# An attention backward pass on one core: sums of Z in halves, Z behind the transposes in two iterations, row factors later, one more transposed block moved

## The chip, the cores and the metric

The kernel runs on one core of a Trainium2 chip, in one launch. The metric is the device time of that core in microseconds. Three runs of the kernel before took 2179.84, 2180.33 and 2181.2 us; the median is 2180.33 us.

## What is computed

The kernel returns the output of one layer and the gradients of its inputs and weights. The layer is an attention (32 heads of 16 channels, 2048 positions, model width 512) gated by a small MLP:

```python
def _fwd_reference(A_x, A_wqkv, A_wo, B_x, B_w1, B_b1, B_w2, B_b2):
    x = A_x
    xn = _layernorm(x, axis=-1)
    s = _A_ref(xn, A_wqkv, A_wo)        # attention, H = 32, Dh = 16, softmax over 2048 keys
    g = _silu(_B_ref(xn, B_w1, B_b1, B_w2, B_b2))
    return x + s * g

def reference(A_x, A_wqkv, A_wo, B_w1, B_b1, B_w2, B_b2, B_x, grad_out):
    ...
    _out, _vjp = jax.vjp(_f, A_x, A_wqkv, A_wo, B_w1, B_b1, B_w2, B_b2)
    _grads = _vjp(grad_out)
    _out0 = jnp.asarray(_out)
    return (_out0, *[jnp.asarray(_g) for _g in _grads])
```

The part that the change touches is the attention core: for each head the scores, their exponentials, the attention output, and the gradients of queries, keys and values, without the 2048 x 2048 matrices ever going to memory whole.

## The kernel before, in words

Three stages follow each other: a first one (class Pre) with projections, layer norms and the MLP, the attention core (attention_core, from line 1051), and a last one (class Grads) with the weight gradients. In the trace the attention core takes from about 218 us to 1852 us.

The attention core has 64 **blocks**, one for each pair of heads (16) and chunk of 512 queries (4). A block has 16 **iterations**, one for each 128 keys. The loop at line 1364 runs over g = 16 * block + iteration; "iteration 5" below means g % 16 == 5. The order of instructions on every engine is the order in which this loop emits them; nothing reorders them. In iteration g TensorE does, in this order:

- `d` and `s` (lines 1137 and 1115): two products of 32 rows by 128 columns each, d (the gradient of the probabilities) for iteration g, s (the scores) for iteration g+1. The four start nearly together, in different row groups of the array, in the order d, s, s, d. There is one buffer for s and there are three for d.
- `Z` (line 1334, emit_z at 1387): four products of 128 rows by 32 columns. They add up the gradients of keys and values of an older block, eight iterations for one half of its keys (z_unit, line 1096). ZOFF = -20 says how far Z trails: unit g - 20. There is one buffer for Z.
- `X` (lines 1232, 1235, 1239): three groups of four products of 128 rows by 32 (17) columns, for iteration g-1. The last group ("g", line 1239) reads `gts`, which VectorE makes. In iteration 1 the "g" group is put off to iteration 2.
- `tT` (lines 1192 and 1196): transposes of 128 x 128 for iteration g-1, seven of them as a rule. `cut` (line 1176) leaves out three in steps 0 and 5 of a block, where two transposes of `xs` (line 1266) take their place in the same buffer; `OLDER` (line 1174) says in which later step each block left out is made up for, as an eighth transpose. There is one buffer for tT.

ScalarE does in each iteration the exponential of s(g+1) (line 1124) and then the copy of the transposes tT of step g-1 into `ek` (line 1208). VectorE does two products gts = d * ets (line 1155, in emit_mult, hj = 0 and hj = 1), and between them at certain iterations a copy of X (emit_xs, iteration 0) or the sum of Z into `acc` (emit_acc, lines 1346 and 1348, iterations 3 and 11 with ZOFF = -20). Ahead of the two products stand the copy of a made-up block into `ek` (emit_cO, line 1215, two iterations after its step's number in OLDER), and in iterations 2 and 7 the copy of transposed xs (line 1274) with, in iteration 2, the reciprocal of the row sums `rL` (line 1294). GpSimd copies one block of ets into gts (line 1153) and makes the row factors W1, W2 that are the weights of Z, and the block's outputs (emit_fin, lines 1295 to 1313). The sync engine's queue transposes gts into `gk` by DMA (line 1172).

After the last block the loop goes on for 20 more iterations that hold the rest of Z and a few products of the last stage (tail_mid).

Of the kernel before, what the change touches and what calls it, by code (L numbers as in the profile page):

```python
# [11 lines left out]
ALU = mybir.AluOpType  # L12
# [1038 lines left out]
def attention_core(ctx, ctx_r, tc, k, grads, Oall, dQall, dKVT_out, ident_f32, ident_bf, npairs=16, nqc=4):  # L1051
    nc = tc.nc
# [37 lines left out]
    blk = [dict(Gk={}, Ek={}) for _ in range(NB)]  # L1090
    cur = {}

    def a_unit(g):
        return (g // 16, g % 16) if 0 <= g < NSTEP else None

    def z_unit(g):
        j = g // 16
        m = g % 8
        return (j, (g % 16) // 8, m if m < 4 else 7 - m, m // 4) if 0 <= j < NB else None
# [41 lines left out]
    def emit_mult(g):  # L1141
        a = a_unit(g)
        if a is None:
            emit_xs(g - 1)
            emit_acc(g + ZOFF)
            return
        kb = a[1]
        if kb % 2 == 0:
            cur["gts"] = gtp.tile([128, 2, 9, 128], bf16, name="gts")
        gts = cur["gts"]  # L1150
        st_gt[g] = gts
        b = 7 * (1 - kb // 4 % 2)
        nc.gpsimd.tensor_copy(out=gts[:, kb % 2, 8, :], in_=st_et[g][:, b // 2, b % 2, :])  # L1153
        for hj in range(2):
            nc.vector.tensor_tensor(out=gts[:, kb % 2, 4 * hj:4 * hj + 4, :],  # L1155
                                    in0=st_d.pop((g, hj))[:].rearrange("k (b q) -> k b q", b=4),
                                    in1=st_et[g][:, :, hj, :], op=ALU.mult)
            if hj == 0:
                emit_xs(g - 1)
                emit_acc(g + ZOFF)  # L1160

    def emit_dmat(g):
        a = a_unit(g)
# [7 lines left out]
            gk = blk[j]["Gk"][kc][:, kb % 4 - 1:kb % 4 + 1]  # L1171
            nc.sync.dma_start_transpose(out=gk.rearrange("q r x k -> q (r x) k"), in_=st_gt[g][:].rearrange("k a x q -> k (a x q)"))

    OLDER = {4: (0, 0), 6: (0, 1), 7: (0, 2), 8: (5, 0), 12: (5, 1), 13: (5, 2)}

    def cut(g):
        return 3 if g >= 16 and g % 16 in (0, 5) else 0

    def older(g):
        return OLDER.get(g % 16) if 16 <= g < NSTEP else None  # L1180

# [91 lines left out]
        j, h = f  # L1273
        nc.vector.tensor_copy(out=blk[j]["xs"][:, 256 * h:256 * h + 256], in_=blk[j].pop("XT"))

    def emit_fin(g):
        f = fin_half(g)
        if f is None:
            return
        j, half = f  # L1280
        p, qc = blocks[j]
        NQq = k.op0["NATQq"]
        NQd = k.op0["NATQd"]
        xf = blk[j]["xs"][:]
        XE = xf[:, 0:256].rearrange("q (b h c) -> q b h c", b=4, h=2)
        XG = xf[:, 256:512].rearrange("q (b h c) -> q b h c", b=4, h=2)
        W1, W2 = WT[j % 2]
        st0 = qc * 4
        nqs = NQq[:, st0:st0 + 4, :, :]
        ndo = NQd[:, st0:st0 + 4, :, :]  # L1290
        bc = lambda ap: ap.to_broadcast([128, 4, 2, 16])
        if half == 1:
            rL = finp.tile([128, 4, 2, 1], f32, name="rL")
            nc.vector.reciprocal(out=rL[:], in_=XG[:, :, :, 17:18])  # L1294
            nc.gpsimd.tensor_tensor(out=W2[:, :, :, 16:32], in0=nqs, in1=bc(rL[:]), op=ALU.mult)  # L1295
            ndl = finp.tile([128, 4, 2, 1], f32, name="ndl")
            nc.gpsimd.tensor_tensor(out=ndl[:], in0=XG[:, :, :, 0:1], in1=rL[:], op=ALU.mult)
            ndr = finp.tile([128, 4, 2, 1], f32, name="ndr")
            nc.gpsimd.tensor_tensor(out=ndr[:], in0=ndl[:], in1=rL[:], op=ALU.mult)
            nc.gpsimd.tensor_tensor(out=W1[:, :, :, 0:16], in0=ndo, in1=bc(rL[:]), op=ALU.mult)  # L1300
            nc.gpsimd.tensor_tensor(out=W1[:, :, :, 16:32], in0=nqs, in1=bc(ndr[:]), op=ALU.mult)
            blk[j]["r"] = rL, ndl
            return
        rL, ndl = blk[j].pop("r")
        Ov = Oall[:, st0:st0 + 4, p * 32:(p + 1) * 32].rearrange("q b (h c) -> q b h c", h=2)
        nc.gpsimd.tensor_tensor(out=Ov, in0=XE[:, :, :, 16:32], in1=bc(rL[:]), op=ALU.mult)
        t1 = finp.tile([128, 4, 2, 16], f32, name="t1")
        nc.gpsimd.tensor_tensor(out=t1[:], in0=XE[:, :, :, 0:16], in1=bc(ndl[:]), op=ALU.mult)
        nc.gpsimd.tensor_tensor(out=t1[:], in0=XG[:, :, :, 1:17], in1=t1[:], op=ALU.add)
        rL4 = finp.tile([128, 4, 2, 1], f32, name="rL4")  # L1310
        nc.gpsimd.tensor_scalar(out=rL4[:], in0=rL[:], scalar1=0.25, scalar2=None, op0=ALU.mult)
        dQv = dQall[:, st0:st0 + 4, p * 32:(p + 1) * 32].rearrange("q b (h c) -> q b h c", h=2)
        nc.gpsimd.tensor_tensor(out=dQv, in0=t1[:], in1=bc(rL4[:]), op=ALU.mult)
        blk[j].pop("xs")

    def emit_z(g):
        u = z_unit(g)
        if u is None:
            return
        j, kp, qb, part = u  # L1320
        if part == 0 and qb == 0:
            blk[j]["Z"] = ps_z.tile([128, 512], f32, name="Z", tag="z")
        Z = blk[j]["Z"]
        for par in range(2):
            kc = 2 * kp + par
            for hj in range(2):
                r = 64 * par + 32 * hj
                if part == 0:
                    mv = blk[j]["Gk"][kc][:, :, 4 * hj + qb, :]
                elif 2 * qb + hj == 7 * (1 - par):  # L1330
                    mv = blk[j]["Gk"][kc][:, :, 8, :]
                else:
                    mv = blk[j]["Ek"][kc][:, :, 2 * qb + hj - par, :]
                nc.tensor.matmul(Z[r:r + 32, :], lhsT=WT[j % 2][1 - part][:, qb, hj, :], rhs=mv,  # L1334
                                 start=(part == 0 and qb == 0), stop=(part == 1 and qb == 0), tile_position=(0, r))

    def emit_acc(g):
        u = z_unit(g)
        if u is None or u[2] != 0 or u[3] != 1:
            return  # L1340
        j, kp = u[0], u[1]
        p, qc = blocks[j]
        Z = blk[j]["Z"]
        av = acc[:, kp, :]
        if qc == 0:
            nc.vector.tensor_copy(out=av, in_=Z[:])
        else:
            nc.vector.tensor_tensor(out=av, in0=Z[:], in1=av, op=ALU.add)  # L1348
        if qc == nqc - 1:
            ob = (outp.tile([128, 512], bf16, name="ob") if kp == 0 or j < NB - 1 else  # L1350
                  xsp.tile([128, 512], bf16, name="ob", tag="xs"))
            nc.gpsimd.tensor_copy(out=ob[:], in_=av)
            dv = dKVT_out[p * 64:(p + 1) * 64, :].rearrange("r (a b s) -> r a b s", a=2, b=2)
            for b in range(2):
                nc.gpsimd.dma_start(out=dv[:, kp, b, :], in_=ob[b * 64:(b + 1) * 64, :])

    FIN_AT = {1: 1, 6: 0}
    FIN_END = {1: 1, 2: 0}
    ZOFF = -20
    late = []  # L1360
    for hj in range(2):
        emit_s(0, hj)
    emit_exp(0)
    for g in range(NSTEP - ZOFF):
        cur["g"] = g
        a = a_unit(g)
        if a is not None:
            j, kb = a
            p, qc = blocks[j]
            if kb == 0 and qc == 0:  # L1370
                L = natq_loads(k, k.op0, p, nc.gpsimd.dma_start) if p > 0 else []
                if p + 1 < npairs:
                    L += op_load_list(k, OP[(p + 1) % 2], p + 1, nc.gpsimd.dma_start)
                else:
                    L += grads.tail_loads(nc.gpsimd.dma_start)
                for i, f in enumerate(L):
                    late.append((g + 16 * (i // 4) + 6 + 3 * (i % 4), f))
        emit_cO(g - 2)
        if a_unit(g - 2) is not None:
            emit_xt(g - 1)  # L1380
            emit_fin(g - 1)
        emit_d(g, 0)
        emit_s(g + 1, 0)
        emit_s(g + 1, 1)
        emit_d(g, 1)
        emit_exp(g + 1)
        emit_z(g + ZOFF)
        emit_x(g - 1, "e")
        emit_x(g - 1, "l")
        if g % 16 == 2:  # L1390
            emit_x(g - 2, "g")
        if g % 16 != 1:
            emit_x(g - 1, "g")
        st_T.pop(g - 2, None)
        emit_T(g - 1)
        emit_XT(g)
        emit_mult(g)
        if a_unit(g - 1) is None:
            emit_xt(g)
            emit_fin(g)  # L1400
        for it in [x for x in late if x[0] <= g]:
            late.remove(it)

            nc.gpsimd.tensor_copy(out=tick[:], in_=st_gt[g][0:1, kb % 2, 7, 126:128])  # L1404
            it[1]()
        if g >= NSTEP:
            grads.tail_mid(g - NSTEP)
        emit_cT(g - 1)
        emit_dmat(g)
        st_gt.pop(g - 3, None)  # L1410
        st_et.pop(g - 12, None)
        if g == NSTEP:
            ctx_r.close()
            grads.tail_open(ps_t, ps_s, ps_d)
# [113 lines left out]
```

## Time and profile before

| | |
|---|---|
| median of three runs | 2180.33 us |
| the profiled execution's own time | 2180.46 us |
| its span in the profile | 2178.8 us |
| granted TensorE clock, mean | 0.997 |
| attention core, first d to last Z | about 218 to 1852 us |
| one block (16 iterations) | about 25.3 us |
| TensorE busy from 800 to 1200 us | 400.00 of 400 us |
| VectorE busy there | 373.57 us |
| ScalarE busy there | 368.38 us |
| GpSimd busy there | 169.99 us |

The span is the time from the first to the last instruction of the profiled execution; 1.7 us of its own time lie around it. A busy TensorE is not a TensorE at its peak: matmuls are pipelined, their ends are modelled, and a wait that is shorter than the tail of the matmul before it does not show as idle time. What the profile's lines hold: start in us from the span's start, duration in us, engine, line of the kernel, operation, output <- inputs, shapes, and xN for N instructions shown as one.

### The profile page before, as it was taken

The page shows a single profiled execution, that of the slowest core. Times are in us where ns is not written, and L with a number is a line of the kernel's source. Part 1 is how long each engine was busy: PE and PEld are TensorE (multiplying, and loading weights), DVE is VectorE, ACT ScalarE, POOL GpSimd, SP SyncE. Part 2 cuts the span into 40 slices and gives each one's busy share as a digit, 9 for nine tenths or more (in the row PEclk, how much of TensorE's full clock was granted, in tenths as well). Part 3 has the DMA queues.
Part 4 walks back from the last instruction along what each step waited for, and adds up shares of the span by engine and source line. Part 5 has one row for each costly group of instructions (what it writes and reads, how often), then busy time and mean ns, then how long its engine had stood idle before and what let it go on. Part 6 is the DMA issues. An engine that isn't in the chain of part 4 may idle for free.

```text
span 2178.8 us, 74934 instructions
## 1 busy us (share of the span) xinstructions
PE 2133.0 (98%) x30659; PEld 1170.6 (54%) x30659; DVE 1898.0 (87%) x3523; ACT 1782.2 (82%) x2481; POOL 870.6 (40%) x2397
## 2 busy tenths in 40 slices
PE   6999999999999999999999999999999999899999
PEld 3444555555555555555555555555555555444444
DVE  6677899999999999999999999999999998788647
ACT  5664899999999999999999999999999997775224
POOL 4376434343434444343434344444434343511003
PEclk9999999999999999999999999999999999999999
DMA  7786999999999999999999999999999999999975
GB/s 235 248 281 202 205 199 198 209 195 200 208 204 198 209 201 201 202 200 206 203 199 201 202 203 201 204 203 204 200 202 206 194 213 212 294 251 240 246 209 178
DMA packets 1416569, 461.17 MB, mean 212 GB/s; under 512 B 1329118, under 2 KB 1400414, under 8 KB 1416224
## 3 DMA queue, kind: packets, MB, share of 16 engines
q1 hardware_dynamic: 1401920, 425.44, 100.3%
q0 software_dynamic: 12720, 29.37, 4.9%
q8 instruction: 240, 3.93, 0.8%
q10 hardware_dynamic: 1584, 1.57, 0.2%
q14 instruction: 105, 0.86, 0.1%
HBM read 62.79 MB, written 64.75 MB: 59 GB/s over the span
## 4 chain that ended last, share of the span: by engine, by line
PE 94%; DVE 2%; DMA 1%; ACT 1%; POOL 0%; issue 0%; SPq 0%; DVEq 0%; ACTq 0%; POOLq 0%
PE tT L1192 22%; PE Z L1334 15%; PE d L1137 15%; PE X L1239 6%; PE X L1232 5%; PE X L1235 5%; PE s L1115 3%; PE ps_dy L909 2%; PE ps_dw L742 2%; PE ps_dw L983 2%; PE ps_h L352 2%; PE ps_m L367 2%; PE ps_dh L875 2%; PE tT L1266 1%; PE ps_dxa L1027 1%; PE ps_dwkv L827 1%
## 5 line engine op out<-in xcount | busy, mean ns | idle before, releaser
L1155 DVE TENSOR_TENSOR gts<-d,ets 128x512 bf16<-128x512 f32 x2048 | 1302.2, 682 | 18.2 <-PE d L1137 3.9
L1124 ACT ACTIVATE ets<-s 128x1024 bf16<-128x1024 f32 x1024 | 1051.6, 1027 | 15.2 <-PE d L1137 3.9
L1208 ACT COPY ek<-tT 128x448 f32<-128x448 f32 (+1 forms) x1024 | 525.1, 513 | 115.0 <-PE tT L1192 31.3
L1192 PE MATMUL tT<-ident_bf,ets 128*128 128x128 bf16 x6790 | 557.9, 221 | 0.0
L1192 PEld LDWEIGHTS <-ets 128*128 128x128 bf16 x6790 | 382.5, 98 | 210.5 <-issue 195.2
L1137 PE MATMUL d<-QDT,KVT 32*128 32x512 bf16 x2048 | 469.4, 384 | 0.0
L1153 POOL COPY gts<-ets 128x128 bf16<-128x128 bf16 x1024 | 281.6, 297 | 387.5 <-ACT ets L1124 382.7
L1115 PE MATMUL s<-QDT,KVT 32*128 32x512 bf16 x2048 | 401.1, 379 | 2.4 <-ACT ets L1124 2.4
L1334 PE MATMUL Z<-gk,W 128*32 128x512 bf16 x2304 | 302.9, 389 | 1.4 <-DVE acc L1348 1.3
L1239 PE MATMUL X<-gts,NAT 128*17 128x256 bf16 x4096 | 290.6, 273 | 0.0
L1232 PE MATMUL X<-ets,NAT 128*32 128x256 bf16 x4096 | 290.4, 273 | 0.0
L1235 PE MATMUL X<-ets,Lc 128*32 128x256 bf16 x4096 | 290.3, 273 | 0.0
L1334 PEld LDWEIGHTS <-W 128*32 128x32 bf16 x4096 | 105.5, 93 | 238.2 <-issue 225.0
L1137 PEld LDWEIGHTS <-KVT 32*128 32x128 bf16 x2048 | 148.5, 91 | 114.3 <-issue 21.5
L1334 PE MATMUL Z<-ek,W 128*32 128x512 bf16 x1792 | 203.6, 389 | 0.0
L1235 PEld LDWEIGHTS <-Lc 128*32 128x32 bf16 x4096 | 110.1, 97 | 108.6
L1215 DVE COPY ek<-tT 128x64 f32<-128x64 f32 x378 | 84.9, 225 | 89.5 <-ACT ek L1208 76.0
L1404 POOL COPY tick<-gts 1x2 bf16<-1x2 bf16 x205 | 36.0, 175 | 313.5 <-DVE gts L1155 313.5
L1115 PEld LDWEIGHTS <-KVT 32*128 32x128 bf16 x2048 | 142.7, 91 | 12.3 <-issue 6.4
L1239 PEld LDWEIGHTS <-NAT 128*17 128x17 bf16 x4096 | 114.7, 91 | 15.4 <-issue 1.1
L1232 PEld LDWEIGHTS <-NAT 128*32 128x32 bf16 x4096 | 108.8, 96 | 5.1 <-issue 5.1
L1295 POOL TENSOR_TENSOR W<-NATQq,rL 128x128 bf16<-128x128 bf16 x64 | 25.5, 399 | 147.9 <-DVE rL L1294 110.3
(252 smaller groups left out, 2470.4 us busy)
## 6 DMA issues: line engine op xcount, KB each, us to landing
gk<-gts SPq DMA_TRANSPOSE x512, 5.6
H1T_s<-h1r SPq DMA_DIRECT2D x28, 256.0 KB, 4.2
HGT_s<-hgT SPq DMA_DIRECT2D x8, 896.0 KB, 4.5
DH_s<-stg SPq DMA_DIRECT2D x12, 512.0 KB, 3.3
hch<-DH_s SPq DMA_DIRECT2D x12, 512.0 KB, 4.8
gp<-H1T_s SPq DMA_DIRECT2D x9, 512.0 KB, 6.8
out_dram<-ob_w POOLq DMA_DIRECT2D x36, 128.0 KB, 4.6
NAT_s<-NS SPq DMA_DIRECT2D x4, 1056.0 KB, 6.1
```

The costliest lines, as they stand in the source:

```text
L1115: nc.tensor.matmul(s[:, hj, :], lhsT=op["KVT"][r:r + 32, kb * 128:(kb + 1) * 128], rhs=op["QDT"][r:r + 32, qc * 512:(qc + 1) * 512], start ...
L1124: nc.scalar.activation(out=st_et[g].rearrange("k b h q -> k h b q"), in_=cur["s"][:].rearrange("k h (b q) -> k h b q", b=4), func=ACT.Exp)
L1137: nc.tensor.matmul(d[:], lhsT=op["KVT"][r:r + 32, kb * 128:(kb + 1) * 128], rhs=op["QDT"][r:r + 32, qc * 512:(qc + 1) * 512], start=True, ...
L1153: nc.gpsimd.tensor_copy(out=gts[:, kb % 2, 8, :], in_=st_et[g][:, b // 2, b % 2, :])
L1155: nc.vector.tensor_tensor(out=gts[:, kb % 2, 4 * hj:4 * hj + 4, :], in0=st_d.pop((g, hj))[:].rearrange("k (b q) -> k b q", b=4), in1=st_et ...
L1192: nc.tensor.transpose(tb[:, i - cut(g), :], et[:, b // 2, b % 2, :], ident_bf[:])
L1208: nc.scalar.copy(out=blk[j]["Ek"][kb // 4][:, kb % 4, c:7].rearrange("q i k -> q (i k)").bitcast(f32), in_=st_T[g][:, 0:(7 - c) * 64])
L1215: nc.vector.tensor_copy(out=blk[g // 16]["Ek"][kk // 4][:, kk % 4, i].bitcast(f32), in_=st_T[g][:, 448:512])
L1232: nc.tensor.matmul(X[r:r + 32, 0:256], lhsT=NATt[:, kb, hj, 1:33], rhs=ev, start=(kb == 0), stop=False, skip_group_check=True, tile_positi ...
L1235: nc.tensor.matmul(X[r:r + 32, 256:512], lhsT=Lc[:], rhs=ev, start=False, stop=False, skip_group_check=True, tile_position=(0, r))
L1239: nc.tensor.matmul(X[r:r + 17, 256:512], lhsT=NATt[:, kb, hj, 0:17], rhs=gv, start=False, stop=(kb == 15), skip_group_check=True, tile_pos ...
L1334: nc.tensor.matmul(Z[r:r + 32, :], lhsT=WT[j % 2][1 - part][:, qb, hj, :], rhs=mv, start=(part == 0 and qb == 0), stop=(part == 1 and qb = ...
```

## The change

Five things, all in the attention core:

1. ZOFF goes from -20 to -21: all of Z comes one iteration later, and the last Z of a half of the keys falls in iterations 4 and 12. The loop after the last block has 21 iterations.
2. The sum of Z into acc, one VectorE instruction over 512 columns in iterations 3 and 11, becomes two over 256 columns each: the first between the two products of iterations 4 and 12, the second between those of 5 and 13.
3. In iterations 5 and 13 the four Z of the next half of the keys are emitted behind the transposes (and behind the products of VectorE) instead of ahead of X.
4. The reciprocal rL moves from the start of VectorE's work in iteration 2 to between the two products of iteration 3; GpSimd's row factors are issued in two parts, in iterations 3 and 4 (and the outputs in 8 and 9).
5. One more block of transposes is left out: `cut` is 1 in step 1, so that six transposes instead of seven stand in iteration 2. It is made up for in step 8; the block that was made up for there goes to step 9, whose transposes are issued in iteration 10. ScalarE's copy in iteration 2 is 64 columns shorter, and VectorE has one more copy (line 1215), in iteration 11.

The diff, without the parts that only pass names on:

```diff
@@ emit_mult
-            emit_acc(g + ZOFF)
+            emit_acc(g + ZOFF, 0)
+            emit_acc(g + ZOFF, 1)
             return
...
             if hj == 0:
                 emit_xs(g - 1)
-                emit_acc(g + ZOFF)
+                emit_acc(g + ZOFF, 0)
+                emit_acc(g - 1 + ZOFF, 1)
+                if a_unit(g - 2) is not None:
+                    emit_fin(g - 2, 0)
...
-    OLDER = {4: (0, 0), 6: (0, 1), 7: (0, 2), 8: (5, 0), 12: (5, 1), 13: (5, 2)}
+    OLDER = {4: (0, 0), 6: (0, 1), 7: (0, 2), 8: (1, 0), 9: (5, 0), 12: (5, 1), 13: (5, 2)}
 
     def cut(g):
-        return 3 if g >= 16 and g % 16 in (0, 5) else 0
+        return {0: 3, 1: 1, 5: 3}.get(g % 16, 0) if g >= 16 else 0
...
+    def z_last(g):
+        u = z_unit(g)
+        return u is not None and u[2] == 0 and u[3] == 1
+
+    def emit_acc(g, h):
+        if not z_last(g):
+            return
...
+        ah, zh = av[:, 256 * h:256 * h + 256], Z[:, 256 * h:256 * h + 256]
         if qc == 0:
-            nc.vector.tensor_copy(out=av, in_=Z[:])
+            nc.vector.tensor_copy(out=ah, in_=zh)
         else:
-            nc.vector.tensor_tensor(out=av, in0=Z[:], in1=av, op=ALU.add)
+            nc.vector.tensor_tensor(out=ah, in0=zh, in1=ah, op=ALU.add)
...
-    ZOFF = -20
+    ZOFF = -21
...
             emit_xt(g - 1)
-            emit_fin(g - 1)
...
-        emit_z(g + ZOFF)
+        z_behind = a is not None and z_last(g - 1 + ZOFF)
+        if not z_behind:
+            emit_z(g + ZOFF)
         emit_x(g - 1, "e")
         emit_x(g - 1, "l")
...
         emit_mult(g)
+        if a_unit(g - 3) is not None:
+            emit_fin(g - 3, 1)
+        if z_behind:
+            emit_z(g + ZOFF)
```

More of the change, by code (lines that the diff above doesn't have):

```diff
@@ L1274, in emit_xt, with emit_fin @@
         nc.vector.tensor_copy(out=blk[j]["xs"][:, 256 * h:256 * h + 256], in_=blk[j].pop("XT"))
-    def emit_fin(g):
+    def emit_fin(g, ph):
         f = fin_half(g)
@@ L1291, in emit_fin @@
         bc = lambda ap: ap.to_broadcast([128, 4, 2, 16])
-        if half == 1:
+        if half == 1 and ph == 0:
             rL = finp.tile([128, 4, 2, 1], f32, name="rL")
@@ L1299, in emit_fin @@
             nc.gpsimd.tensor_tensor(out=ndr[:], in0=ndl[:], in1=rL[:], op=ALU.mult)
+            blk[j]["r"] = rL, ndl, ndr
+            return
+        if half == 1:
+            rL, ndl, ndr = blk[j]["r"]
             nc.gpsimd.tensor_tensor(out=W1[:, :, :, 0:16], in0=ndo, in1=bc(rL[:]), op=ALU.mult)
             nc.gpsimd.tensor_tensor(out=W1[:, :, :, 16:32], in0=nqs, in1=bc(ndr[:]), op=ALU.mult)
-            blk[j]["r"] = rL, ndl
             return
-        rL, ndl = blk[j].pop("r")
+        rL, ndl, ndr = blk[j]["r"]
         Ov = Oall[:, st0:st0 + 4, p * 32:(p + 1) * 32].rearrange("q b (h c) -> q b h c", h=2)
-        nc.gpsimd.tensor_tensor(out=Ov, in0=XE[:, :, :, 16:32], in1=bc(rL[:]), op=ALU.mult)
+        if ph == 0:
+            nc.gpsimd.tensor_tensor(out=Ov, in0=XE[:, :, :, 16:32], in1=bc(rL[:]), op=ALU.mult)
+            return
         t1 = finp.tile([128, 4, 2, 16], f32, name="t1")
@@ L1335, in emit_z @@
                                  start=(part == 0 and qb == 0), stop=(part == 1 and qb == 0), tile_position=(0, r))
-    def emit_acc(g):
+    def z_last(g):
         u = z_unit(g)
-        if u is None or u[2] != 0 or u[3] != 1:
+        return u is not None and u[2] == 0 and u[3] == 1
+    def emit_acc(g, h):
+        if not z_last(g):
             return
+        u = z_unit(g)
         j, kp = u[0], u[1]
@@ L1344, in emit_acc @@
         av = acc[:, kp, :]
+        ah, zh = av[:, 256 * h:256 * h + 256], Z[:, 256 * h:256 * h + 256]
         if qc == 0:
-            nc.vector.tensor_copy(out=av, in_=Z[:])
+            nc.vector.tensor_copy(out=ah, in_=zh)
         else:
-            nc.vector.tensor_tensor(out=av, in0=Z[:], in1=av, op=ALU.add)
-        if qc == nqc - 1:
+            nc.vector.tensor_tensor(out=ah, in0=zh, in1=ah, op=ALU.add)
+        if qc == nqc - 1 and h == 1:
             ob = (outp.tile([128, 512], bf16, name="ob") if kp == 0 or j < NB - 1 else
@@ L1397, in attention_core @@
         emit_mult(g)
+        if a_unit(g - 3) is not None:
+            emit_fin(g - 3, 1)
+        if z_behind:
+            emit_z(g + ZOFF)
         if a_unit(g - 1) is None:
             emit_xt(g)
-            emit_fin(g)
+            emit_fin(g, 0)
+            emit_fin(g, 1)
         for it in [x for x in late if x[0] <= g]:
```

## Prediction

> **What bounds the kernel now.** I read the page first: which engine is full, and of whom the chain that ended last is made.
>
> ```profile
> span 2178.8 us, 74934 instructions
> PE 2133.0 (98%) x30659; PEld 1170.6 (54%) x30659; DVE 1898.0 (87%) x3523; ACT 1782.2 (82%) x2481; POOL 870.6 (40%) x2397
> PE 94%; DVE 2%; DMA 1%; ACT 1%; POOL 0%; issue 0%; SPq 0%; DVEq 0%; ACTq 0%; POOLq 0%
> ```
>
> TensorE is busy 98% and makes up 94% of the chain, so on this view only its queue counts. But a wait shorter than a matmul's tail doesn't show, so next I read the timeline, engine by engine, of one block (iteration 2 starts at 1007.52). TensorE, to the start of iteration 6:
>
> ```profile
> 1007.64 0.39 PE L1115 MATMUL s<-QDT,KVT 32*128 32x512 bf16 x2
> ...
> 1008.73 0.56 PE L1192 MATMUL tT<-ident_bf,ets 128*128 128x128 bf16 x7
> 1009.23 0.39 PE L1137 MATMUL d<-QDT,KVT 32*128 32x512 bf16 x1
> 1009.23 0.39 PE L1115 MATMUL s<-QDT,KVT 32*128 32x512 bf16 x2
> 1009.34 0.37 PE L1137 MATMUL d<-QDT,KVT 32*128 32x512 bf16 x1
> ...
> 1010.80 0.39 PE L1137 MATMUL d<-QDT,KVT 32*128 32x512 bf16 x1
> 1010.84 0.39 PE L1115 MATMUL s<-QDT,KVT 32*128 32x512 bf16 x2
> ...
> 1011.61 0.40 PE L1239 MATMUL X<-gts,NAT 128*17 128x256 bf16 x4
> ...
> 1012.45 0.38 PE L1137 MATMUL d<-QDT,KVT 32*128 32x512 bf16 x1
> 1012.45 0.39 PE L1115 MATMUL s<-QDT,KVT 32*128 32x512 bf16 x2
> 1012.46 0.39 PE L1137 MATMUL d<-QDT,KVT 32*128 32x512 bf16 x1
> 1012.77 0.40 PE L1334 MATMUL Z<-gk,W 128*32 128x512 bf16 x4
> 1013.00 0.28 PE L1232 MATMUL X<-ets,NAT 128*32 128x256 bf16 x4
> ...
> 1013.21 0.28 PE L1239 MATMUL X<-gts,NAT 128*17 128x256 bf16 x4
> 1013.43 0.56 PE L1192 MATMUL tT<-ident_bf,ets 128*128 128x128 bf16 x7
> 1013.83 0.22 PE L1196 MATMUL tT<-ident_bf,ets 128*128 128x128 bf16 x1
> 1013.98 0.39 PE L1137 MATMUL d<-QDT,KVT 32*128 32x512 bf16 x1
> 1014.06 0.39 PE L1115 MATMUL s<-QDT,KVT 32*128 32x512 bf16 x2
> ```
>
> What to see: s does not always follow d at once (0.04 late at 1010.84, 0.08 at 1014.06). ScalarE's exponentials say why:
>
> ```profile
> 1008.12 1.02 ACT L1124 ACTIVATE ets<-s 128x1024 bf16<-128x1024 f32 x1
> ...
> 1009.76 1.03 ACT L1124 ACTIVATE ets<-s 128x1024 bf16<-128x1024 f32 x1
> ...
> 1011.33 1.03 ACT L1124 ACTIVATE ets<-s 128x1024 bf16<-128x1024 f32 x1
> ...
> 1012.98 1.03 ACT L1124 ACTIVATE ets<-s 128x1024 bf16<-128x1024 f32 x1
> ```
>
> s has one buffer. From s at 1007.64 to its exponential at 1008.12 are 0.48; it takes 1.03; the next s can start 0.05 after its end (1009.76 + 1.03 = 1010.79, s at 1010.84). So **s cannot come more often than every 1.56 us**, whatever TensorE saves; an iteration takes 1.58 on average (25.3 / 16). What the change can win is about 16 x 0.02 = 0.3 us per block, while a delay of TensorE beyond that ring counts in full. I follow the starts of s.
>
> VectorE's timeline has the two waits that the change is aimed at, and the durations that price it:
>
> ```profile
> 1008.04 0.41 DVE L1274 COPY xs<-tT 128x256 f32<-128x256 f32 x1
> 1008.49 0.21 DVE L1294 RECIPROCAL rL<-xs 128x8 f32<-128x8 f32 x1
> ...
> 1010.40 0.68 DVE L1348 TENSOR_TENSOR acc<-Z,acc 128x512 f32<-128x512 f32 x1
> 1011.00 0.68 DVE L1155 TENSOR_TENSOR gts<-d,ets 128x512 bf16<-128x512 f32 x1
> ...
> 1012.93 0.69 DVE L1155 TENSOR_TENSOR gts<-d,ets 128x512 bf16<-128x512 f32 x1
> ...
> 1013.54 0.68 DVE L1155 TENSOR_TENSOR gts<-d,ets 128x512 bf16<-128x512 f32 x1
> ```
>
> The sum at 1010.40 pushes the second gts of iteration 3 to 1011.00, with its end at 1011.68; the X of iteration 4 that reads it takes 0.40 instead of 0.28: TensorE waits 0.12. In iteration 3 the second d starts 0.11 after the first, because rL and the copy ahead of it delayed the gts that frees its buffer.
>
> **The change part by part.** Iteration by iteration, with s before and after; iteration 2 starts as before.
>
> Row factors and the block left out (iterations 2 to 4). One transpose less is one step of 0.06 ((1013.83 - 1013.43) / 7), so d of iteration 3 comes at 1009.17. Its s waits for the exponential: 1008.12 + 1.02 + 0.05 = 1009.19 or 1009.20, before 1009.23. With rL gone from iteration 2 the second d no longer waits: 1009.20, before 1009.34. From a second d over seven transposes to the next first d are 1.46 (1009.34 to 1010.80): iteration 4 starts at 1010.66. Its s, by the ring, at 1009.20 + 1.56 = 1010.76, before 1010.84. The same again: d of iteration 5 at 1010.77 + 1.46 = 1012.23 (the X there no longer waits, as the sum is gone from iteration 3), s at 1012.32, **before 1012.45: 0.13 won**. TensorE itself won more (0.22); the ring takes the rest.
>
> GpSimd's factors cost nothing: the page has it busy 40%, and W2 is first read at the end of iteration 5, W1 in iteration 9. On SP's queue nothing moves; Z reads its transposes an iteration later than before. On VectorE rL and a first half sum lie between the products of iterations 3 and 4, where s waits for the ring anyway; if that cover went, the second gts of iteration 4 would hold X of iteration 5. It ends by 1010.66 + 0.49 + 0.61 + 0.34 + 0.68 = 1012.78 (0.34 for a half's turn: half of the sum's 0.60 plus a fixed part), plus 0.05; X "g" reads it at 1012.97.
>
> Z behind the transposes (iteration 5). Without Z ahead of it X follows d at 0.31 (1012.46 to 1012.77): 1012.64; transposes 0.43 later (1013.00 to 1013.43) at 1013.07; eight of them and the turn to other work take 0.55 (1013.43 to 1013.98): Z could start at **1013.62**. But the first Z overwrites the buffer that the second half sum reads, and that stands on VectorE behind a gts which waits for d of this iteration: 0.49 from d to gts (1012.45 to 1012.93), 0.61 to the next turn (1012.93 to 1013.54), then the half sum. No row shows it; the lower bound is the 64-column copy, the upper the whole sum.
>
> ```profile
> L1215 DVE COPY ek<-tT 128x64 f32<-128x64 f32 x378 | 84.9, 225 | 89.5 <-ACT ek L1208 76.0
> ...
> L1346 DVE COPY acc<-Z x32: 678/681/682, 264.1 to 1795.5; 128x512 f32<-128x512 f32 x32
> ```
>
> That is 0.23 to 0.68. I take 0.41, the 256-column copy at 1008.04, since at 512 columns copy and sum are equal (0.68). The last link is VectorE's end to Z's start; the one place where Z waits for a sum shows it (0.05: 1846.67 to 1846.72), and what follows a Z in another array shape is in the same tail:
>
> ```profile
> 1845.99 0.68 DVE L1348 TENSOR_TENSOR acc<-Z,acc 128x512 f32<-128x512 f32 x1
> ...
> 1846.72 1.05 PE L1334 MATMUL Z<-gk,W 128*32 128x512 bf16 x16 [0.29 <-DVE acc L1348]
> ...
> 1850.98 0.38 PE L1334 MATMUL Z<-ek,W 128*32 128x512 bf16 x1
> 1851.29 0.39 PE L584 MATMUL ps_so<-wo_sb,oT 128*128 128x512 bf16 x1
> ```
>
> So Z starts 0.49 + 0.61 + 0.41 + 0.05 = 1.56 after d, at 1013.79, and TensorE has stood 0.17. Behind it comes d of iteration 6. Z to d is not in the trace: Z to X, in the same array shape (128*32), takes 0.23 (1012.77 to 1013.00); Z to a 128*128 product 0.31; d to Z 0.31. As d has another shape (32*128), I take 0.31, plus 0.01 for the four starts. **Iteration 5 takes 1.56 + 0.32 = 1.88**, and d and s of iteration 6 come at 1014.11, before 1014.06: from 0.13 ahead to 0.05 behind.
>
> The Trainium skill, TensorEngine Tiling (Array Packing), section Key Properties, says that changing the tiling mode (not just the tile) drains TensorE. That speaks against this change: Z ahead of X costs no change of mode of its own, Z between transposes and d costs one. By this rule the sum is as above; without it, it is the second rival's.
>
> The extra transpose (iteration 10). TensorE gets back the 0.06; s is late there anyway (d to s 0.08 to 0.09 in the iterations after, as at 1014.06), so only about 0.02 comes through, by way of ScalarE's copy that starts later. VectorE's added copy (0.23) falls in an iteration where it idles: 89.5 us ahead of 378 such copies, 0.24 each.
>
> Iterations 12 and 13. Before, s to s is 1.60:
>
> ```profile
> 1025.01 0.39 PE L1115 MATMUL s<-QDT,KVT 32*128 32x512 bf16 x2
> ...
> 1026.61 0.39 PE L1115 MATMUL s<-QDT,KVT 32*128 32x512 bf16 x2
> ```
>
> After, iteration 13 has the chain of iteration 5: 1.88 from d to d. Its own s stands 0.08 behind d (by the ring), the next one at d: 1.80 from s to s, **0.20 lost**. The wait of X on the sum in iteration 12 goes, but the ring holds s there.
>
> Sum per block: 0.05 + 0.02 + 0.20 = 0.27 us. Z stands behind in iteration 13 of block 1 and twice in blocks 2 to 63: 125 times, 62.5 pairs, 62.5 x 0.27 = 16.9 us. In the tail two Z wait for two halves (at most 0.41 + 0.41) instead of 0.68: up to 0.14 each, 0.3 in all. On the profiled execution's own time, 2180.46 (span 2178.8 plus 1.7 around it): **2197.7 us**, +0.8%. That execution is 0.13 over the median of the runs, which I leave aside.
>
> **The rivals.**
>
> The half sum is in time (the other side: not slower). Place: the end of iterations 5 and 13. It decides where the half sum ends 0.17 sooner, as with its lower bound of 0.23: then Z follows the transposes at once, each iteration takes 1.71, and the block comes to 0.27 - 0.34 = -0.07: 62.5 x -0.07 + 0.3 = -4.1, 2176.4 us. For it: nothing shows a half sum. Against: the 256-column copy, at 0.41.
>
> Z to d costs what Z to X costs, 0.23. Then each of the 125 is 0.09 shorter: 16.9 - 11.3 + 0.3 = 5.9, 2186.4 us. The Trainium skill, TensorE: Matmul & The Clock Gate, section Architectural detail, says that TensorE's queue can pull weight loads ahead of matmuls in flight; that would give this time. Against: all three changes of shape in the rows (d to Z, Z to 128*128, X to transposes with 0.22 for 256 columns) cost some 0.1 over the stream.
>
> VectorE becomes the bound. It gets 0.34 + 0.34 - 0.60 = 0.08 per sum and one copy, 0.15 + 0.23 = 0.38 per block. If none of it fell into idle time, 64 x 0.38 = 24 on top of the forecast's: up to 2222 us; half of it 2210. Against: its 87%, and the idle time ahead of the copies.
>
> The change doesn't act: the waits only change place and all stays as it was, 2180 us. Against: 1.88 is longer than the longest gain.
>
> **How the numbers follow.** Forecast 0.70, its own range 2192 to 2204 (0.03 either way on the 0.41 and the 0.32 of 125 places is 7 us, less at the top as a longer wait there eases the ring). Half sum in time 0.07; Z to d cheap 0.10; VectorE the bound 0.08; no effect 0.05. 0.2% is 4.4 us, about what a measurement of this kernel can tell from no change. The forecast, VectorE and nearly all of the cheap turn are slower; the half sum in time lies on the edge of faster. Faster 0.06, same 0.09, slower 0.85. Leaving out the in-time case, no effect and the far end of VectorE's, the range is 2186 to 2207; with a half sum of 0.68 it would be 34 us more, which equal rows for copy and sum exclude.
>
> **What would show it.** In the profile after: iteration 5 and 13 at about 1.88 from d to d, Z there waiting for acc and starting 1.56 after d, d 0.31 behind the last Z; half sums of 0.41; second d of iteration 3 close behind s; no 0.40 on line 1239 in iteration 4; s to s otherwise 1.55 to 1.58. Wrong if Z in 5 and 13 starts before 1.45 after d, if d follows it by 0.23, or if s to s falls under 1.54 anywhere.

## The result and the profile after

The changed kernel takes 2210.01 us (2208.79 to 2211.53 in four runs), the kernel before 2180.09 (2176.09 to 2181.2): a ratio of 1.0142, with a 95% interval of 1.013 to 1.0155. The change costs 30 us. The forecast was 2197.7 and its range ended at 2207: the direction and the place were right, the size was 12 us short.

The page of the changed kernel, with the lines that answer to those of before:

```profile
span 2208.1 us, 75141 instructions
PE 2148.3 (97%) x30610; PEld 1185.7 (54%) x30659; DVE 1921.7 (87%) x3714; ACT 1791.1 (81%) x2481; POOL 876.2 (40%) x2397
PE 85%; DVE 8%; DMA 3%; issue 1%; ACT 1%; POOL 1%; SPq 0%; DVEq 0%; ACTq 0%; POOLq 0%
```

TensorE's share of the chain falls from 94% to 85%, VectorE's rises from 2% to 8%. Busy shares hardly move: TensorE is still 97% busy, because the wait hides under the tails of its matmuls (below, the last transpose is booked until 1258.67 and Z starts at 1258.76).

An iteration 5 of the changed kernel on TensorE, with the d of iteration 4 ahead of it; d comes at 1257.14, the next d at 1259.09:

```profile
1255.57 0.39 PE L1137 MATMUL d<-QDT,KVT 32*128 32x512 bf16 x1
...
1257.14 0.39 PE L1137 MATMUL d<-QDT,KVT 32*128 32x512 bf16 x1
1257.21 0.39 PE L1115 MATMUL s<-QDT,KVT 32*128 32x512 bf16 x2
...
1257.76 0.36 PE L1243 MATMUL X<-gts,NAT 128*17 128x256 bf16 x4
1258.05 0.56 PE L1196 MATMUL tT<-ident_bf,ets 128*128 128x128 bf16 x7
1258.45 0.22 PE L1200 MATMUL tT<-ident_bf,ets 128*128 128x128 bf16 x1
1258.76 0.40 PE L1343 MATMUL Z<-gk,W 128*32 128x512 bf16 x4
1259.09 0.38 PE L1137 MATMUL d<-QDT,KVT 32*128 32x512 bf16 x1
1259.10 0.39 PE L1115 MATMUL s<-QDT,KVT 32*128 32x512 bf16 x2
```

and VectorE in iterations 4 (d at 1255.57) and 5:

```profile
1256.16 0.69 DVE L1156 TENSOR_TENSOR gts<-d,ets 128x512 bf16<-128x512 f32 x1 [0.23 <-POOL ndl L1301]
1256.77 0.41 DVE L1362 TENSOR_TENSOR acc<-Z,acc 128x256 f32<-128x256 f32 x1
1257.10 0.68 DVE L1156 TENSOR_TENSOR gts<-d,ets 128x512 bf16<-128x512 f32 x1
1257.70 0.68 DVE L1156 TENSOR_TENSOR gts<-d,ets 128x512 bf16<-128x512 f32 x1
1258.29 0.41 DVE L1362 TENSOR_TENSOR acc<-Z,acc 128x256 f32<-128x256 f32 x1
1258.62 0.68 DVE L1156 TENSOR_TENSOR gts<-d,ets 128x512 bf16<-128x512 f32 x1
```

The last transpose starts at 1258.45, so Z could start 0.15 later, at 1258.60. It starts at 1258.76: the half sum ends at 1258.70. That is no single case: by the medians of blocks 4 to 61, Z starts 0.31 behind the last transpose and 0.05 behind the end of the half sum, in iteration 5 and in iteration 13. The chain of waits of the same stretch (start, duration, what) says it as a sequence, and where it came from:

```profile
1257.20 0.32 PE d L1137
...
1257.70 0.68 DVE gts L1156
1258.38 0.34 DVE acc L1362
1258.72 0.04 issue
1258.76 0.40 PE Z L1343 x4
1259.16 0.32 PE d L1137
```

To compare whole blocks, here is the time from one s to the next, in ns, as the median over blocks 4 to 61, worked out from the starts of s in the two traces:

```
iteration   2    3    4    5    6    7    8    9   10   11   12   13   14   15    0    1
before   1594 1610 1607 1610 1551 1575 1575 1575 1575 1551 1551 1595 1556 1596 1552 1552
after    1551 1570 1552 1887 1585 1551 1599 1552 1598 1553 1552 1890 1585 1563 1552 1552
```

Iterations 2 to 4 win 138 ns, iteration 5 loses 277, iterations 6 to 12 lose 37, iterations 13 to 1 lose 291: 467 ns per block by these medians, 62.5 times 0.467 = 29.2 us. Single blocks scatter about the medians, so that this is a little too much: from the first d to the last d are 1647.96 us instead of 1620.36, 27.6 us more.

The rest is behind the last block. In the tail the first sum now stands on VectorE behind two instructions of the last stage. The first Z that waits for it has 1.54 us of idle time ahead of it, where it had 0.29:

```profile
1874.03 0.68 DVE L591 TENSOR_TENSOR t<-ps_so,s1g 128x512 f32<-128x512 f32 x1
1874.63 0.74 DVE L1362 TENSOR_TENSOR acc<-Z,acc 128x256 f32<-128x256 f32 x2
```

```profile
1875.48 0.40 PE L1343 MATMUL Z<-gk,W 128*32 128x512 bf16 x4 [1.54 <-POOL dQall L1322]
```

The profile names GpSimd's dQall as what ended this wait. But dQall had ended at 1874.73 and the second half sum ends at 1875.37, 0.11 before Z starts; in e7 below, Z starts before dQall does.

```profile
1874.33 0.40 POOL L1322 TENSOR_TENSOR dQall<-t,rL 128x128 bf16<-128x128 f32 x1
```

From the last d to the end of the last Z are 14.50 us instead of 12.86: 1.6 us more.

### The profile page after: what moved, and what is told of

Read it like the earlier page. It is cut to its first block, busy times and chain, and to the rows that moved or that the text cites. A ratio compares the mean times of both kernels' runs of the same rounds, so it can differ in the third digit from the quotient of the medians.

```text
span 2208.1 us, 75141 instructions
## 1 busy us (share of the span) xinstructions
PE 2148.3 (97%) x30610; PEld 1185.7 (54%) x30659; DVE 1921.7 (87%) x3714; ACT 1791.1 (81%) x2481; POOL 876.2 (40%) x2397
## 3 DMA queue, kind: packets, MB, share of 16 engines
q10 hardware_dynamic: 1584, 1.57, 0.2%
## 4 chain that ended last, share of the span: by engine, by line
PE 85%; DVE 8%; DMA 3%; issue 1%; ACT 1%; POOL 1%; SPq 0%; DVEq 0%; ACTq 0%; POOLq 0%
PE tT L1196 19%; PE Z L1343 15%; PE d L1137 15%; PE X L1236 4%; PE X L1243 4%; PE X L1239 4%; DVE gts L1156 4%; PE s L1115 3%; PE ps_dy L909 2%; PE ps_dw L983 2%; PE ps_dw L742 2%; PE ps_h L352 2%; PE ps_m L367 2%; PE ps_dh L875 2%; DMA gk<-gts 2%; DVE acc L1362 1%
## 5 line engine op out<-in xcount | busy, mean ns | idle before, releaser
L1156 DVE TENSOR_TENSOR gts<-d,ets 128x512 bf16<-128x512 f32 x2048 | 1326.8, 682 | 37.2 <-POOL ndl L1301 14.2
L1212 ACT COPY ek<-tT 128x448 f32<-128x448 f32 (+2 forms) x1024 | 521.7, 509 | 88.5 <-PE tT L1196 6.1
L1196 PE MATMUL tT<-ident_bf,ets 128*128 128x128 bf16 x6727 | 554.4, 221 | 0.0
L1154 POOL COPY gts<-ets 128x128 bf16<-128x128 bf16 x1024 | 293.2, 295 | 540.4 <-ACT ets L1124 535.9
L1137 PE MATMUL d<-QDT,KVT 32*128 32x512 bf16 x2048 | 464.6, 385 | 0.0
L1343 PEld LDWEIGHTS <-W 128*32 128x32 bf16 x4096 | 116.3, 93 | 227.0 <-issue 185.7
L1137 PEld LDWEIGHTS <-KVT 32*128 32x128 bf16 x2048 | 152.7, 91 | 129.9 <-issue 50.0
L1219 DVE COPY ek<-tT 128x64 f32<-128x64 f32 x441 | 99.2, 225 | 61.5 <-ACT ek L1212 38.9
L1115 PEld LDWEIGHTS <-KVT 32*128 32x128 bf16 x2048 | 146.6, 91 | 10.0 <-issue 5.2
L1200 PE MATMUL tT<-ident_bf,ets 128*128 128x128 bf16 x441 | 96.6, 219 | 0.0
```

The costliest lines, as they stand in the source:

```text
L1115: nc.tensor.matmul(s[:, hj, :], lhsT=op["KVT"][r:r + 32, kb * 128:(kb + 1) * 128], rhs=op["QDT"][r:r + 32, qc * 512:(qc + 1) * 512], start ...
L1137: nc.tensor.matmul(d[:], lhsT=op["KVT"][r:r + 32, kb * 128:(kb + 1) * 128], rhs=op["QDT"][r:r + 32, qc * 512:(qc + 1) * 512], start=True, ...
L1196: nc.tensor.transpose(tb[:, i - cut(g), :], et[:, b // 2, b % 2, :], ident_bf[:])
L1212: nc.scalar.copy(out=blk[j]["Ek"][kb // 4][:, kb % 4, c:7].rearrange("q i k -> q (i k)").bitcast(f32), in_=st_T[g][:, 0:(7 - c) * 64])
L1219: nc.vector.tensor_copy(out=blk[g // 16]["Ek"][kk // 4][:, kk % 4, i].bitcast(f32), in_=st_T[g][:, 448:512])
```

## The experiments

The theory from the two traces: the loss is the wait of Z for the second half sum in iterations 5 and 13, and the half sum is later than forecast because the first gts of iterations 4 and 12 starts 0.1 late, which VectorE carries into the next iteration. Rivals: the place of Z behind the transposes is the loss, whatever it waits for; VectorE's added instructions are; GpSimd's factors (`ndl`, the name in the wait above) hold that gts. Each run below was measured beside the kernel before on its own chip, whose medians were 2178.07 to 2179.97 us there; a difference between two changed versions that is given in us compares medians of different chips, and can be off by about 2 us.

**e4_small_copy: why the first product of iterations 4 and 12 is late.**

```diff
+        if kb in (4, 12):
+            nc.vector.tensor_copy(out=tick2[:], in_=st_et[g][0:1, 0, 0, 0:2])
         for hj in range(2):
             nc.vector.tensor_tensor(out=gts[:, kb % 2, 4 * hj:4 * hj + 4, :],
```

`tick2` is a tile of two elements that nothing reads.

> The changed kernel with one VectorE copy of 1x2 elements more, in iterations 4 and 12 ahead of the products, that reads ets and so takes the wait for ScalarE off the product behind it. Theory (the first product of these iterations starts 0.1 late, because its waits for TensorE, a DMA, ScalarE and GpSimd are taken one after the other by two queue instructions and the product): it starts 0.48 to 0.50 after d in iteration 4 instead of 0.59, that of iteration 5 at 0.49 instead of 0.56; iteration 5 takes 1.89, iteration 13 1.92; 2203 us. Rival (GpSimd's small factors ndl hold that product, as the wait's name says): iteration 4 stays at 0.59, 2210 us. Rival (VectorE's load): one instruction more twice per block, 2213 us.

It took 2202.61 us, against 2178.8 for the kernel before on the same chip: 1.0107 (1.0087 to 1.0127). VectorE in iteration 4 (d at 1251.85) and the first product of iteration 5 (d at 1253.42):

```profile
1252.12 0.15 DVE L1157 COPY tick<-ets 1x2 bf16<-1x2 bf16 x1
1252.33 0.69 DVE L1159 TENSOR_TENSOR gts<-d,ets 128x512 bf16<-128x512 f32 x1
...
1253.91 0.69 DVE L1159 TENSOR_TENSOR gts<-d,ets 128x512 bf16<-128x512 f32 x1
```

and GpSimd there:

```profile
1252.15 0.21 POOL L1304 TENSOR_TENSOR ndl<-xs,rL 128x8 f32<-128x8 f32 x1
```

The product starts 0.48 after d instead of 0.59, with one instruction more ahead of it, and before ndl ends (1252.36): ndl did not hold it. The first product of iteration 5 then starts 0.49 after d instead of 0.56. By the medians, the small copy takes less in iteration 12 (0.53 instead of 0.58), and the product of iteration 13 starts at 0.51. Iterations 5 and 13 take 1.90 each (forecast here 1.89 and 1.92) instead of 1.95 and 1.96. In the trace of the changed kernel VectorE's queue has two semaphore instructions ahead of that product; the first ends its wait for TensorE 0.45 after d, the second, with the waits for a DMA and ScalarE, then starts at 0.50 and takes 0.05, and the product starts at 0.59. In e4 the small copy has taken one of the waits before d is done. That the waits are taken one after the other fits both traces; that it is their number alone was not tried in another way. What is shown: without ScalarE's wait on it the product starts 0.11 earlier, and 7 us come back.

**e3_half_first: does Z wait for the half sum, or is its place the loss?**

```diff
-                emit_acc(g - 1 + ZOFF, 1)
...
+        emit_acc(g - 1 + ZOFF, 1)
         for hj in range(2):
             nc.vector.tensor_tensor(out=gts[:, kb % 2, 4 * hj:4 * hj + 4, :],
```

> The changed kernel with the second half sum ahead of both products of VectorE in iterations 5 and 13 instead of between them; Z stays behind the transposes. Theory (Z waits for the half sum, which stands behind a product that waits for d): the half sum ends about 1.0 after d, Z starts behind the transposes at about 1.46, iterations 5 and 13 take 1.80 instead of 1.95; 0.16 less at 125 places, 2190 us. Rival (the place of Z behind the transposes, with its change of array shape, is nearly all of the loss): within 4 us of 2210. Rival (VectorE's added instructions): 2210, as their number is the same.

It took 2191.76 us, 1.0055 (1.0034 to 1.0075). Iteration 5 (d at 1244.84) on TensorE:

```profile
1246.15 0.22 PE L1200 MATMUL tT<-ident_bf,ets 128*128 128x128 bf16 x1
1246.30 0.40 PE L1343 MATMUL Z<-gk,W 128*32 128x512 bf16 x4
1246.63 0.39 PE L1137 MATMUL d<-QDT,KVT 32*128 32x512 bf16 x1
```

Z follows the transposes at 0.15, with no wait, and the iteration takes 1.79. 18 us come back with the same instructions in the same number. So the wait of Z for the half sum is most of the loss, and neither the place alone nor VectorE's load is.

**e12_both: both at once.** The edits of e3 and e4 together.

> The changed kernel with both of e3_half_first (second half sum ahead of the products of iterations 5 and 13) and e4_small_copy (the wait for ScalarE taken off the first product of iterations 4 and 12). Theory: the first product of iteration 4 starts at 0.48 after d, X of iteration 5 no longer waits for gts, Z follows the transposes without a wait; iterations 5 and 13 take 1.72 to 1.74, s to s 1.66; 2183 to 2186 us. What is left over the kernel before is then the change of array shape behind Z and the tail. Rival (e3 and e4 win the same wait): 2190 us.

It took 2182.0 us against 2179.97: 1.0012 (1.0003 to 1.0022). Iteration 5, from one d to the next:

```profile
1241.65 0.39 PE L1138 MATMUL d<-QDT,KVT 32*128 32x512 bf16 x1
...
1242.27 0.28 PE L1246 MATMUL X<-gts,NAT 128*17 128x256 bf16 x4
...
1243.04 0.40 PE L1346 MATMUL Z<-gk,W 128*32 128x512 bf16 x4
1243.37 0.39 PE L1138 MATMUL d<-QDT,KVT 32*128 32x512 bf16 x1
```

X takes 0.28 (0.36 in the changed kernel: it waited for gts), Z does not wait, the iteration takes 1.72. With both mended, 28 of the 30 us are back. What the change was aimed at does not come out as a gain: from s to s iterations 5 and 13 still take 1.65 and 1.66, before 1.61 and 1.60. By these medians iterations 5 and 13 (0.11 per block), iterations 6 and 14 (0.06) and the tail take what iterations 2 to 4 and iteration 15 win. For iterations 5 and 13 the change of array shape behind Z has the right size (0.33 from Z to d here, 0.23 from Z to X before, twice per block); it was not tried by itself.

**e2_whole: whole sums, Z ahead of X.**

```diff
-        z_behind = a is not None and z_last(g - 1 + ZOFF)
+        z_behind = False
...
-                emit_acc(g + ZOFF, 0)
-                emit_acc(g - 1 + ZOFF, 1)
+                emit_acc(g + ZOFF, 1, 512)
```

> The changed kernel with the sum of Z whole again (512 columns, between the two products of iterations 4 and 12) and Z ahead of X in all iterations; ZOFF -21, row factors and the left-out block as in the change. Theory (the second half sum in the next iteration, and Z waiting for it, is the loss): iterations 5 and 13 fall from 1.95 to about 1.65 to 1.73, s to s there 1.64 to 1.66, no Z waits for a sum, X waits about 0.1 for the whole sum instead; 2180 us, within 5. Rival (VectorE's added instructions are the loss): only 0.15 us per block comes back, 2200 us.

It took 2185.75 us, 1.0031 (1.0014 to 1.0048). From s to s iterations 5 and 13 take 1.66 and 1.67, as forecast: there X waits for the gts behind the whole sum.

```profile
1247.75 0.40 PE L1241 MATMUL X<-gts,NAT 128*17 128x256 bf16 x4
```

24 of the 30 us come back without the halves. It ends 7 us over the kernel before, a little outside what was expected: I had left out the tail, whose wait it keeps (14.32 from the last d to the last Z), and from s to s iterations 6 and 14, behind the late ones, take 1.61 (before 1.55 and 1.56).

**e5_rl_back: the row factors alone taken back.**

```diff
-                if a_unit(g - 2) is not None:
-                    emit_fin(g - 2, 0)
...
             emit_xt(g - 1)
+            emit_fin(g - 1, 0)
```

> The changed kernel with the reciprocal rL back at the start of VectorE's work in iteration 2 (the outputs' first part comes one iteration earlier too); all else as changed. Theory (the ring s, exponential, s sets the time there): the second d of iteration 3 waits about 0.09 again, but s of iteration 4 and 5 waits for the ring anyway; 2210 us, within 2. Rival (the row factors' place is worth what TensorE no longer waits): 0.09 x 63 blocks, 2215 us.

It took 2219.12 us, 1.0186 (1.0169 to 1.0203): 9 us more than the changed kernel, and my expectation fell. Iteration 3, to the start of iteration 4:

```profile
1286.32 0.38 PE L1137 MATMUL d<-QDT,KVT 32*128 32x512 bf16 x1
1286.34 0.39 PE L1115 MATMUL s<-QDT,KVT 32*128 32x512 bf16 x2
1286.49 0.37 PE L1137 MATMUL d<-QDT,KVT 32*128 32x512 bf16 x1
...
1287.95 0.39 PE L1137 MATMUL d<-QDT,KVT 32*128 32x512 bf16 x1
1287.95 0.39 PE L1115 MATMUL s<-QDT,KVT 32*128 32x512 bf16 x2
```

With one transpose less in iteration 2, d comes earlier but the gts that frees the second d's buffer doesn't: the second d waits 0.15, not 0.09. That is more than the ring's slack: s to s is 1.62 where the changed kernel has 1.57, by the medians. The loss goes on behind it: iteration 4 takes 1.61 (1.55 in the changed kernel) and iteration 5 1.91 (1.89), 0.13 per block in all, or 8 of the 9 us. In the changed kernel, then, the left-out block needs the row factors' move.

**e6_no_cut: the left-out block alone taken back.**

```diff
-    OLDER = {4: (0, 0), 6: (0, 1), 7: (0, 2), 8: (1, 0), 9: (5, 0), 12: (5, 1), 13: (5, 2)}
+    OLDER = {4: (0, 0), 6: (0, 1), 7: (0, 2), 8: (5, 0), 12: (5, 1), 13: (5, 2)}
...
-        return {0: 3, 1: 1, 5: 3}.get(g % 16, 0) if g >= 16 else 0
+        return {0: 3, 5: 3}.get(g % 16, 0) if g >= 16 else 0
```

> The changed kernel without the one more block left out (seven transposes in iteration 2, six made-up blocks). Theory: s of iteration 3 comes 0.04 later and stays so, 0.02 come back in iterations 10 and 11; 0.02 to 0.04 per block, 2211 to 2213 us. Rival (the added copy on VectorE costs): 2206 us or less.

It took 2211.37 us, 1.0154 (1.0137 to 1.0171), inside the expectation and, at 1.4 us from the changed kernel, not to be told apart from it. That VectorE's copy cost something, the rival, is not borne out: without it, and with the seventh transpose back in iteration 2, the kernel is no faster.

**e7_tail: the order in the tail.**

```diff
-        if n == 3:
+        if n == 4:
             self.emit_so(1)
             self.emit_oT(3)
```

> The changed kernel with the second of two products of the last stage that stand among the last Z (emit_so(1) with emit_oT(3)) one iteration later, behind the sum that the next Z waits for. Theory (2.1 us of the loss are in the tail: with Z one iteration later the first sum there stands on VectorE behind two instructions of that product, and Z waits 1.54 us instead of 0.29): Z waits under 0.5 us there, the time from the last d to the end falls by 1 to 2 us; 2208.5 us. Rival (the tail grew by the 21st iteration and the halves): no change, 2210 us.

The Z that waited 1.54 us now has 0.18 ahead of it, and the last Z ends 13.04 us after the last d instead of 14.50:

```profile
1877.01 1.05 PE L1343 MATMUL Z<-gk,W 128*32 128x512 bf16 x16 [0.18 <-PE o_tp L575]
```

The order was the cause of the longer tail. In the time it can't be seen: 2207.84 us, 1.0131 (1.011 to 1.0153), 2.2 us under the changed kernel with intervals that overlap; the last stage behind the tail varies by several us from run to run (336 to 343 us from the last d to the end in these traces).

**e8_rl_head: is there a gain in the row factors for the kernel before?** rL at the head of iteration 3, ahead of both products.

```diff
             emit_xt(g - 1)
-            emit_fin(g - 1)
+            for x in (g - 1, g - 2):
+                if fin_half(x) and fin_half(x)[1] == g - 1 - x:
+                    emit_fin(x)
```

> The kernel before (ZOFF -20, whole sums in iterations 3 and 11) with only the reciprocal rL and the row factors moved to the head of iteration 3, ahead of both products, where VectorE would wait for d. Theory: the second d of iteration 3 no longer waits, X of iteration 4 waits about 0.09 instead of 0.12, but the ring takes most of it: 0.05 per block, 2177 us. Rival (no effect, the ring takes all): 2180 us. Rival (GpSimd's work behind a later rL delays W2 for Z of iteration 4): 2183 us or more.

2176.65 us against 2178.07: 0.999 (0.9979 to 1.0002). The profiles agree with the theory (25.25 us per block, 25.31 before); the times are also in keeping with no effect.

**e9_rl_head_cut: and the left-out block with it.** The edit of e8, and OLDER and cut as in the change.

> The same with one more block left out in iteration 2 (made up for in iterations 9 and 10, as in the change). Theory: s of iteration 3 comes 0.04 earlier and keeps it, s of iteration 5 about 0.12, less 0.02 in iterations 10 and 11: 0.10 per block, 2174 us. Rival (the ring takes all): 2180 us. Rival (VectorE's added copy costs): 2182 us or more.

2193.49 us, 1.0068 (1.0054 to 1.0082): 19 us over the expectation. The sum of Z is still in iteration 11 here, and the left-out block puts a copy ahead of it there (d of iteration 11 at 1259.98):

```profile
1260.64 0.23 DVE L1215 COPY ek<-tT 128x64 f32<-128x64 f32 x1
1260.79 0.68 DVE L1155 TENSOR_TENSOR gts<-d,ets 128x512 bf16<-128x512 f32 x1
1261.38 0.68 DVE L1348 TENSOR_TENSOR acc<-Z,acc 128x512 f32<-128x512 f32 x1
```

```profile
1261.50 0.38 PE L1137 MATMUL d<-QDT,KVT 32*128 32x512 bf16 x1
...
1261.60 0.38 PE L1137 MATMUL d<-QDT,KVT 32*128 32x512 bf16 x1
1262.12 0.40 PE L1334 MATMUL Z<-gk,W 128*32 128x512 bf16 x4
...
1262.55 0.45 PE L1239 MATMUL X<-gts,NAT 128*17 128x256 bf16 x4
...
1263.43 0.38 PE L1137 MATMUL d<-QDT,KVT 32*128 32x512 bf16 x1
```

The copy waits for ScalarE until 0.66 after d; the sum behind it ends at 1262.06, and Z of iteration 12 comes 0.52 after the second d (1261.60) instead of 0.31, and X takes 0.45. Iteration 12 takes 1.93 instead of 1.60. It is the changed kernel's loss again, in another place: a sum that stands behind a late product, with Z behind the sum.

**e11_rl_head_cut10: the same, with the copy in iteration 12.**

```diff
-    OLDER = {4: (0, 0), 6: (0, 1), 7: (0, 2), 8: (5, 0), 12: (5, 1), 13: (5, 2)}
+    OLDER = {4: (0, 0), 6: (0, 1), 7: (0, 2), 8: (1, 0), 10: (5, 0), 12: (5, 1), 13: (5, 2)}
```

> The kernel before with the row factors at the head of iteration 3 and one more block left out, as in e9_rl_head_cut, but the made-up block that fell there in step 9 (VectorE's copy in iteration 11, beside the whole sum) goes to step 10, so that the copy stands in iteration 12. Theory (in e9_rl_head_cut the copy's wait for ScalarE held the sum of iteration 11 and X of iteration 12 behind it, 1.93 instead of 1.60): iteration 12 is back at about 1.55 to 1.60, s of iteration 5 comes 0.06 earlier than in e8_rl_head, 0.04 per block in all; 2174 us. Rival (the left-out block itself costs): 2180 us or more.

2172.66 us against 2179.97: 0.9971 (0.9958 to 0.9983). Iteration 12 takes 1.54, and this version beats both kernels, the one before by 0.3%, the changed one, by the medians, by 37 us. So the row factors and the left-out block, parts of the change, are a gain where the whole sum and the place of Z are left as they were.

## Why the prediction was right in direction and short in size

The prediction's steps, with what the runs showed:

- Iterations 2 to 4: 0.13 won by s of iteration 5, measured 0.138. The ring of s, exponential and s takes the rest of what TensorE saves, as said.
- The half sum 0.41: measured 0.41. VectorE's end to Z 0.05: 0.06. Z to d 0.32: 0.33, where Z to X without a change of array shape is 0.23. The Trainium skill, TensorEngine Tiling (Array Packing), Key Properties, says that a change of tiling mode drains TensorE. The 0.10 more agrees with it, though no run here tells a drain from another cost of the change.
- **The step that failed: "0.49 from d to gts" in iterations 5 and 13.** It is 0.56 there. The prediction itself puts a half sum between the products of iteration 4, and started the first of these at 0.49 as well; that one starts at 0.59, so VectorE comes out of iteration 4 0.07 late. Z starts 1.62 after d, not 1.56. The iteration took 1.95 and 1.96 instead of 1.88. e4, which takes that delay away, brings back 7.4 of the 12.3 us that were missing. The trace before had a row for it: in iteration 0 the product has the same four waits ahead of it (TensorE, a DMA, ScalarE, GpSimd) and starts 0.59 after d (1004.43 to 1005.02), where VectorE's turns of 0.60 would have let it start at 0.50. In iterations 4 and 12 before, VectorE was busy until 0.80 and 0.75 after d by the medians, which hid such a wait; the change uncovered it.
- From s to s iterations 5 and 13 lose 0.28 and 0.30, forecast 0.18 and 0.20; 0.07 of the difference in each is that step, and the rest is that s stands 0.07, not 0.08 to 0.09, behind d at their start.
- Iterations 6 and 14, behind them, take 1.59 instead of 1.55 and 1.56, which the forecast left out. Its ring of 1.56 holds for an s that starts behind d; in these iterations s starts beside d and has its exponential 0.51 later (1259.10 to 1259.61), not 0.48. The prediction's own rows show 0.53 for an s beside d (1009.23 to 1009.76, 1012.45 to 1012.98). Iteration 15 wins 0.03 of it back.
- The extra transpose in iteration 10: 0.02 forecast. Iterations 7 to 12 together lost less than 0.01, and e6, without the extra transpose, takes the same time there: it cost next to nothing.
- The tail: at most 0.3 forecast, 1.6 measured. The halves themselves cost what was said; the order on VectorE, which puts the first sum behind the last stage's two instructions, was missed. e7 shows it.

Of the rivals, the half sum in time is what e12 builds: 2182 us, at the edge of no change, where the rival had 2176. A cheap turn from Z to d fell with the 0.33 there, and no effect with the 1.95 and 1.96. VectorE as the bound was given 2210 to 2222, and the time fell there, but by another mechanism: its added work hardly counts (e6 saves a copy and wins nothing; e4 adds two and wins 7 us). The range failed because the start of the longest chain, 0.49 from d to gts, was given no uncertainty. It came from iteration 5 before, where VectorE is done with iteration 4 in time; in the changed kernel a half sum stands in iteration 4 behind a late first product, and VectorE is not.

## What to carry to other kernels

Here a sum cut in two moved its second half behind everything that the next iteration's first product waits for; before cutting one, follow that product's own chain to the instruction that needs the buffer. Move such a half to the head of the next iteration's work, where the engine would wait anyway (e3: 18 us, though no gain over the kernel before). And when a chain is repeated 125 times, each link's start must be read from an iteration with the same instructions and the same waits ahead of it: 0.07 us there was 7 us here (e4).

## What the runs showed that was not expected

In iteration 4 a product of VectorE with waits for TensorE, a DMA, ScalarE and GpSimd starts 0.59 after d, the last of them to come; with ScalarE's taken off by a copy of two elements that itself takes 0.15, it starts 0.48 after d (e4). The exponential follows its s sooner when s runs behind d (0.47: 1257.21 to 1257.68) than when it runs beside it (0.51), so that in this kernel a late s makes up 0.04 by itself:

```profile
1257.68 1.02 ACT L1124 ACTIVATE ets<-s 128x1024 bf16<-128x1024 f32 x1
...
1259.61 1.02 ACT L1124 ACTIVATE ets<-s 128x1024 bf16<-128x1024 f32 x1 [0.36 <-PE d L1137]
```
